# An attention and hard-swish kernel: its fallback path rolled into one loop over the batches, with a shared identity matrix

## The chip, the cores and the metric

The kernel runs on one core of a Trainium2 chip. The metric is the device time of one execution in microseconds (us), as the median of several runs. Beside it stands one profiled execution, whose span reaches from its first to its last recorded instruction.

## What is computed

The input `x` has 4 batches of 12480 rows with 128 channels; there are 32 inducing rows. The reference, cut to what matters:

```python
def mab(q, kv):
    s = scale * (q @ kv.transpose(0, 2, 1))
    s = s - s.max(-1, keepdims=True)
    a = np.exp(s)
    a /= a.sum(-1, keepdims=True) + 1e-09
    return a @ kv
h = mab(I, x)            # 32 inducing rows attend to the 12480 rows of their batch
y = mab(x, h)            # every row attends to the 32 rows of h
u = y.reshape(B * N, 128) @ w_in                       # 128 -> 2048
out = (u * np.clip(u + 3.0, 0.0, 6.0) / 6.0) @ w_out   # 2048 -> 128
```

## The kernel before

The kernel has two paths. The **main path** is straight code, without a loop at run time. It uses that a hard-swish whose argument stays between -3 and 3 is a polynomial of second degree: with the 32 rows of `h` known, the output of a row of `x` is a sum over products of its attention weights, with coefficients that are worked out once for each batch (`c_units`). A batch's 12480 rows are cut into 7 groups (6 of 128 partitions by 16 rows, one of 48 by 4), and the groups into 25 chunks of 4 rows for each partition. A loop written out in Python goes over the 100 chunks of all batches (`t` in `range(total)`); for each it issues the exponentials (`b_base`), the products (`b_prod`), the linear and the quadratic matmuls into one PSUM bank (`b_lin`, `b_quad`, the last at L692), and one chunk later the evacuation (`b_evac`, L708) and, after each group, the output DMA from SP's queue (L715). Between the parts of a chunk a list of units of the next batch is filled in by share (`fill`, `bg`). The inputs come by DMAs from GpSimd's queue (`load_x`, L118).

At the start GpSimd's queue holds the first load of `x`, the two instructions that make the identity (`make_identity`; in the profile they have lines of `masks.py`), four more loads of `x`, and then small constants. The identity is used by one transpose of the inducing rows (L173), by its copy in bf16 (`ident_b`, L162) with which all rows of `x` are transposed, and by the constant `sel` (L194).

At the end the kernel counts in how many places its conditions hold (five VectorE operations at L793 to L806, a matmul at L810, a sum at L812), compares the count with the number wanted and writes `bad_i` (L814), and evacuates the last chunk. All five engines then read `bad_i` into a register (`values_load`, the profile's L818) and branch (`tc.If`, the profile's L821). If a condition failed, they go into the **direct path** (`direct_path`): three loops of 130 tiles of 96 rows for each batch, in float32, which compute the reference as it stands. With the given inputs the conditions hold, and no instruction of the direct path runs.

How this is laid out in the instruction streams matters here. Each engine has its own stream of instructions of 64 bytes, and the order in each is: the main path; the branch into the direct path, which is not taken; a short "else" part, which sets the semaphores to what the direct path would have left them at (`EVENT_SEMAPHORE` at L821) and ends in a second branch, over the direct path to the end; the direct path; the end. In the end (the profile's L966, where the tile context closes) SP waits for every DMA queue and every engine, and then all engines meet twice: each drains and adds to a semaphore, GpSimd waits for the four others and releases them.

The direct path is written out for each batch, since `for b in range(B)` is a Python loop; only the three loops within a batch (`tc.For_i`) are loops at run time. Each of them has, on every engine, a part that is run if it has no iterations, a part between two iterations in which all engines meet and semaphores are set back, and a part behind it that waits for everything. It makes an identity of its own with two GpSimd operations. Counted in the streams that this kernel compiles to (marks of branch targets not counted), the second branch stands at, and the distance from it to the end is:

| engine | place of the second branch | instructions from it to the end | of them for one batch |
|---|---|---|---|
| TensorE | 7917 | 950 | 236 |
| VectorE | 761 | 420 | 104 |
| ScalarE | 575 | 301 | 75 |
| GpSimd | 97 | 306 | 75 |
| SyncE | 241 | 406 | 97 |

The direct path has 19 DMAs, all from SP's queue: three for the weights and the inducing rows, and four for each batch. SP gives its DMAs eight semaphores in turn, S[108] and S[112] to S[118]; the last output DMA of the main path has S[108], and the direct path begins with S[112].

Of the kernel before, what the change touches and what calls it, by code (L numbers as in the profile page):

```python
# [9 lines left out]
FP32 = mybir.dt.float32  # L10
# [30 lines left out]
def kernel(  # L41
# [8 lines left out]
    nc = tc.nc  # L50
    P = nc.NUM_PARTITIONS
    B, N, C = x.shape
# [4 lines left out]
    scale = 1.0 / math.sqrt(C)  # L57
# [18 lines left out]

    keep = ctx.enter_context(tc.tile_pool(name="keep", bufs=1))
    bad_i = keep.tile([1, 1], I32, name="bad_i")

    with ExitStack() as es:  # L80
        es.enter_context(tc.manual_schedule())
        const = es.enter_context(tc.tile_pool(name="const", bufs=1))
# [69 lines left out]
            nc.gpsimd.dma_start(w_out_r[:, :, :], w_out)  # L152


        ident = const.tile([P, P], FP32, name="ident")
        make_identity(nc, ident[:, :])
        for g in range(1, XBUF):
            load_x(0, g)
# [586 lines left out]
        for t in range(total):  # L745
            if t % NCK == 0:
                b = t // NCK
# [71 lines left out]
        bad_i[0:1, 0:1], min_val=0, max_val=1, skip_runtime_bounds_check_because="a comparison gives 0 or 1"  # L819
    )  # L820
    with tc.If(bad > 0, preferred_fallthrough_block=False):  # L821
        direct_path(tc, x, inducing, moe_w_in, moe_w_out, out, scale)


def direct_path(tc, x, inducing, moe_w_in, moe_w_out, out, scale):
    nc = tc.nc
    P = nc.NUM_PARTITIONS
    B, N, C = x.shape
    M = inducing.shape[0]
    F = moe_w_in.shape[1]  # L830
    FB = F // P
    TN = 96
    assert N % TN == 0
    xf = x.rearrange("b n c -> (b n) c")
    PSUM = bass.MemoryType.PSUM
    with ExitStack() as es:
        kp = es.enter_context(tc.tile_pool(name="d_keep", bufs=1))
        wk = es.enter_context(tc.tile_pool(name="d_work", bufs=1))
        ps = es.enter_context(tc.tile_pool(name="d_ps", bufs=1, space=PSUM))
        ident = kp.tile([P, P], FP32, name="d_ident")  # L840
        make_identity(nc, ident[:, :])
        w_in = kp.tile([P, F], FP32, name="d_w_in")
        nc.sync.dma_start(w_in[:, :], moe_w_in[:, :])
        w_out = kp.tile([P, FB, C], FP32, name="d_w_out")
        nc.sync.dma_start(w_out[:, :, :], moe_w_out.rearrange("(kb kp) c -> kp kb c", kp=P))
        I_sb = kp.tile([M, C], FP32, name="d_I")
        nc.sync.dma_start(I_sb[:, :], inducing[:, :])
        I_T = kp.tile([P, M], FP32, name="d_IT")
        tr = ps.tile([P, 512], FP32, name="d_tr")
        nc.tensor.transpose(tr[:, :M], I_sb[:, :], ident[:M, :M])  # L850
        nc.vector.tensor_copy(I_T[:, :], tr[:, :M])

        def load(row):
            xt = wk.tile([TN, C], FP32, name="d_x")
            nc.sync.dma_start(xt[:, :], xf[bass.ds(row, TN), :])
            tr = ps.tile([P, 512], FP32, name="d_tr")
            nc.tensor.transpose(tr[:, :TN], xt[:, :], ident[:TN, :TN])
            xT = wk.tile([P, TN], FP32, name="d_xT")
            nc.vector.tensor_copy(xT[:, :], tr[:, :TN])
            return xt, xT  # L860

        def weights_of(xT):
            s = ps.tile([P, 512], FP32, name="d_s")
            nc.tensor.matmul(s[:M, :TN], lhsT=I_T[:, :], rhs=xT[:, :])
            return s

        for b in range(B):
            mx = kp.tile([M, 1], FP32, name="d_mx")
            nm = kp.tile([M, 1], FP32, name="d_nm")
            D = kp.tile([M, 1], FP32, name="d_D")  # L870
            Ha = kp.tile([M, C], FP32, name="d_Ha")
            HT = kp.tile([P, M], FP32, name="d_HT")
            nc.vector.memset(mx[:, :], -3.0e38)
            nc.vector.memset(D[:, :], 0.0)
            nc.vector.memset(Ha[:, :], 0.0)
            with tc.For_i(b * N, (b + 1) * N, TN) as row:
                xt, xT = load(row)
                s = weights_of(xT)
                m1 = wk.tile([M, 1], FP32, name="d_m1")
                nc.vector.tensor_reduce(m1[:, :], s[:M, :TN], axis=AX.X, op=ALU.max)  # L880
                nc.vector.tensor_max(mx[:, :], mx[:, :], m1[:, :])
            nc.vector.tensor_scalar_mul(nm[:, :], mx[:, :], -scale)
            with tc.For_i(b * N, (b + 1) * N, TN) as row:
                xt, xT = load(row)
                s = weights_of(xT)
                a = wk.tile([M, TN], FP32, name="d_a")
                nc.scalar.activation(a[:, :], s[:M, :TN], ACT.Exp, scale=scale, bias=nm[:, 0:1])
                d1 = wk.tile([M, 1], FP32, name="d_d1")
                nc.vector.tensor_reduce(d1[:, :], a[:, :], axis=AX.X, op=ALU.add)
                nc.vector.tensor_add(D[:, :], D[:, :], d1[:, :])  # L890
                tr = ps.tile([P, 512], FP32, name="d_tr")
                nc.tensor.transpose(tr[:TN, :M], a[:, :], ident[:M, :M])
                aT = wk.tile([TN, M], FP32, name="d_aT")
                nc.vector.tensor_copy(aT[:, :], tr[:TN, :M])
                hp = ps.tile([P, 512], FP32, name="d_h")
                nc.tensor.matmul(hp[:M, :C], lhsT=aT[:, :], rhs=xt[:, :])
                nc.vector.tensor_add(Ha[:, :], Ha[:, :], hp[:M, :C])
            nc.vector.tensor_scalar_add(D[:, :], D[:, :], 1.0e-9)
            nc.vector.reciprocal(D[:, :], D[:, :])
            nc.vector.tensor_scalar_mul(Ha[:, :], Ha[:, :], D[:, 0:1])  # L900
            tr = ps.tile([P, 512], FP32, name="d_tr")
            nc.tensor.transpose(tr[:, :M], Ha[:, :], ident[:M, :M])
            nc.vector.tensor_copy(HT[:, :], tr[:, :M])
            with tc.For_i(b * N, (b + 1) * N, TN) as row:
                xt, xT = load(row)
                s = ps.tile([P, 512], FP32, name="d_s")
                nc.tensor.matmul(s[:TN, :M], lhsT=xT[:, :], rhs=HT[:, :])
                m2 = wk.tile([TN, 1], FP32, name="d_m2")
                nc.vector.tensor_reduce(m2[:, :], s[:TN, :M], axis=AX.X, op=ALU.max)
                nc.vector.tensor_scalar_mul(m2[:, :], m2[:, :], -scale)  # L910
                a = wk.tile([TN, M], FP32, name="d_a2")
                nc.scalar.activation(a[:, :], s[:TN, :M], ACT.Exp, scale=scale, bias=m2[:, 0:1])
                d2 = wk.tile([TN, 1], FP32, name="d_d2")
                nc.vector.tensor_reduce(d2[:, :], a[:, :], axis=AX.X, op=ALU.add)
                nc.vector.tensor_scalar_add(d2[:, :], d2[:, :], 1.0e-9)
                nc.vector.reciprocal(d2[:, :], d2[:, :])
                nc.vector.tensor_scalar_mul(a[:, :], a[:, :], d2[:, 0:1])
                tr = ps.tile([P, 512], FP32, name="d_tr")
                nc.tensor.transpose(tr[:M, :TN], a[:, :], ident[:TN, :TN])
                aT = wk.tile([M, TN], FP32, name="d_aT2")  # L920
                nc.vector.tensor_copy(aT[:, :], tr[:M, :TN])
                hp = ps.tile([P, 512], FP32, name="d_h")
                nc.tensor.matmul(hp[:, :TN], lhsT=Ha[:, :], rhs=aT[:, :])
                h = wk.tile([P, TN], FP32, name="d_hT")
                nc.vector.tensor_copy(h[:, :], hp[:, :TN])
                up = ps.tile([P, FB, P], FP32, name="d_u")
                for jb in range(FB):
                    nc.tensor.matmul(up[:, jb, :TN], lhsT=w_in[:, jb * P : (jb + 1) * P], rhs=h[:, :])
                g = wk.tile([P, FB, TN], FP32, name="d_g")
                nc.vector.tensor_scalar(g[:, :, :], up[:, :, :TN], 3.0, 0.0, op0=ALU.add, op1=ALU.max)  # L930
                nc.vector.tensor_scalar(g[:, :, :], g[:, :, :], 6.0, 1.0 / 6.0, op0=ALU.min, op1=ALU.mult)
                nc.vector.tensor_mul(g[:, :, :], g[:, :, :], up[:, :, :TN])
                op = ps.tile([P, 512], FP32, name="d_o")
                for jb in range(FB):
                    nc.tensor.matmul(
                        op[:TN, :C], lhsT=g[:, jb, :], rhs=w_out[:, jb, :], start=(jb == 0), stop=(jb == FB - 1)
                    )
                ot = wk.tile([TN, C], FP32, name="d_ot")
                nc.vector.tensor_copy(ot[:, :], op[:TN, :C])
                nc.sync.dma_start(out[bass.ds(row, TN), :], ot[:, :])  # L940


# [28 lines left out]
```

## Time and profile before

| what | us |
|---|---|
| median of 5 runs | 328.26 |
| lowest and highest of them | 327.68 and 330.8 |
| profiled execution, its own time | 327.56 |
| its span | 325.8 |
| TensorE busy (matmul) | 301.3 (92% of the span) |
| VectorE, ScalarE, GpSimd busy | 237.9, 229.4, 23.3 |
| mean granted TensorE clock | 0.974 |

The profiled execution took 1.8 us more than its span, which begins with the first and ends with the last instruction. Start times in the profile count from the start of the span. A letter q behind an engine (SPq) is its sequencer: waits on semaphores, branches, register loads and drains are done there and do not count as busy. Queues q8 and q14 of kind "instruction" are those by which the engines' own instructions are brought in: q8 moved 33 packets and 0.54 MB, so 16 KB each, q14 21 packets and 0.17 MB, so 8 KB each.

### The profile page before, as it was taken

The numbers are of one execution on the slowest core, as the hardware profiler recorded it, in microseconds if no ns is written. First come the engines' busy times: TensorE is split into PE (matmuls) and PEld (weight loads), VectorE is DVE, ScalarE is ACT, GpSimd is POOL, SyncE is SP. The second block draws the span as 40 slices with busy tenths as digits, with TensorE's granted clock in tenths as the row PEclk, the third lists the DMA queues.
The fourth block names the chain that finished last, engine by engine and source line by source line (L and its number), as shares of the span: only waits on it lengthen the run. The fifth ranks groups of instructions, "written<-read, shape, count | busy, mean of one in ns | idle before, by whom it ended". The sixth has DMA issues, their size and how long they took to land.

```text
span 325.8 us, 9615 instructions
## 1 busy us (share of the span) xinstructions
PE 301.3 (92%) x3920; PEld 236.3 (73%) x3934; DVE 237.9 (73%) x542; ACT 229.4 (70%) x416; POOL 23.3 (7%) x59
## 2 busy tenths in 40 slices
PE   6798998999799998999999998999999999999980
PEld 2684766888477786898777786898777787777770
DVE  2688766788486776978796776978796777887780
ACT  2582787986459858887579768888489756777720
POOL 8140210101000000110100000100000000000000
PEclk9799997999979999999999999999999999999995
DMA  7999398798855155579984256561654255666642
GB/s 234 409 300 233 76 406 296 261 313 271 330 185 167 44 186 189 150 251 359 319 301 162 65 179 195 143 201 29 195 172 160 61 184 187 196 218 208 196 185 105
DMA packets 26486, 67.78 MB, mean 208 GB/s; under 512 B 5152, under 2 KB 19520, under 8 KB 20288
## 3 DMA queue, kind: packets, MB, share of 16 engines
q1 hardware_dynamic: 18160, 38.36, 36.6%
q0 software_dynamic: 8272, 28.71, 28.3%
q8 instruction: 33, 0.54, 0.6%
q14 instruction: 21, 0.17, 0.2%
HBM read 29.77 MB, written 25.56 MB: 170 GB/s over the span
## 4 chain that ended last, share of the span: by engine, by line
PE 75%; DMA 10%; DVE 7%; ACT 3%; issue 2%; POOL 0%; SPq 0%; DVEq 0%; POOLq 0%
PE op L692 26%; PE bp L652 11%; PE op L676 7%; DMA d<-dk 6%; PE hnd L282 6%; PE pt L260 5%; PE cp L490 4%; PE dpm L470 4%; DMA xr<-in_x_dram 4%; PE s L268 2%; PE pp L623 2%; DVE xT L261 2%; PE sp L593 2%; PE ep L579 2%; DVE TD L668 2%
## 5 line engine op out<-in xcount | busy, mean ns | idle before, releaser
L659 ACT ACTIVATE TF<-bp 128x512 bf16<-128x512 f32 (+1 forms) x200 | 117.9, 600 | 40.3 <-PE rp L612 26.3
L692 PE MATMUL op<-Cq,TF 128*128 128x128 bf16 (+1 forms) x800 | 109.8, 224 | 0.0
L692 PE MATMUL op<-Cq,TD 128*128 128x128 bf16 (+1 forms) x800 | 107.0, 220 | 2.1 <-DVE TD L668 2.1
L708 DVE TENSOR_TENSOR os<-op,r_all 128x512 f32<-128x512 f32 (+1 forms) x100 | 68.3, 683 | 20.5 <-PE op L692 19.6
L692 PEld LDWEIGHTS <-TF 128*128 128x128 bf16 (+1 forms) x800 | 50.9, 98 | 34.2 <-issue 26.0
L668 DVE TENSOR_TENSOR TD<-TF,d 128x1024 bf16<-128x1024 bf16 (+1 forms) x100 | 67.0, 670 | 7.9 <-DMA d<-dk 4.0
L652 PE MATMUL bp<-xT,W 128*128 128x512 bf16 (+1 forms) x189 | 71.7, 380 | 0.0
L692 PEld LDWEIGHTS <-TD 128*128 128x128 bf16 (+1 forms) x800 | 61.9, 99 | 2.5 <-DVE TD L668 2.4
L676 PE MATMUL op<-BD,nf 128*128 128x512 f32 (+1 forms) x100 | 53.5, 535 | 0.0
L251 ACT CAST xb<-xr 128x1024 bf16<-128x1024 f32 (+1 forms) x47 | 46.0, 1002 | 7.1 <-DMA xr<-in_x_dram 7.1
L481 ACT ACTIVATE sq<-dpm 128x512 bf16<-128x512 f32 x60 | 36.5, 645 | 5.2 <-PE dpm L470 3.2
L261 DVE COPY xT<-pt 128x1024 bf16<-128x1024 bf16 (+1 forms) x56 | 33.8, 617 | 8.0 <-PE pt L260 7.8
L613 DVE RECIPROCAL r_all<-rp 128x4 f32<-128x4 f32 (+1 forms) x100 | 17.8, 178 | 24.5 <-PE rp L612 23.9
L612 PE MATMUL rp<-one,nf 128*128 128x4 f32 (+1 forms) x100 | 34.8, 348 | 0.1
L260 PE MATMUL pt<-ident_b,xb 128*128 128x128 bf16 (+1 forms) x400 | 30.9, 223 | 2.3 <-DVE xb L251 1.5
L282 PE MATMUL hnd<-xr,a 128*32 128x128 f32 x384 | 32.2, 231 | 0.5 <-ACT a L274 0.5
L282 PEld LDWEIGHTS hnd<-xr,a 128*32 128x32 f32 x384 | 26.0, 113 | 2.7 <-issue 2.1
L260 PEld LDWEIGHTS <-xb 128*128 128x128 bf16 (+1 forms) x400 | 24.6, 100 | 4.2 <-DVE xb L251 1.6
L118 POOL DMA_DIRECT2D xr<-in_x_dram x25 | 13.5, 543 | 166.2 <-ACT TF L659 97.7
L490 PE MATMUL cp<-w_out_b,sq 128*128 128x128 bf16 x256 | 24.3, 220 | 0.5 <-ACT sq L481 0.4
L630 ACT ACTIVATE dk<-pp 128x512 bf16<-128x512 f32 (+1 forms) x28 | 15.8, 564 | 11.5 <-PE pp L623 10.5
L470 PE MATMUL dpm<-dH,w_in_b 128*128 128x512 bf16 x62 | 22.9, 381 | 0.9 <-DVE dH L400 0.5
(106 smaller groups left out, 344.5 us busy)
## 6 DMA issues: line engine op xcount, KB each, us to landing
out_dram<-os SPq DMA_DIRECT2D x24, 1024.0 KB, 4.1
xr<-in_x_dram POOLq DMA_DIRECT2D x23, 1024.0 KB, 8.0
d<-dk SPq DMA_DIRECT2D x96, 128.0 KB, 4.1
xr<-in_x_dram POOLq DMA_DIRECT2D x2, 512.0 KB, 4.7
w_in_r<-in_moe_w_in_dram POOLq DMA_DIRECT2D x1, 1024.0 KB, 10.1
w_out_r<-in_moe_w_out_dram POOLq DMA_DIRECT2D x1, 1024.0 KB, 14.5
w_in_b<-in_moe_w_in_dram POOLq DMA_DIRECT2D x1, 512.0 KB, 7.1
w_out_b<-in_moe_w_out_dram POOLq DMA_DIRECT2D x1, 512.0 KB, 12.3
```

Of the source, the lines that this page charges most:

```text
L251: eng(xb[:p, lo:hi, :], xs[(b, g)][:p, lo:hi, :].bitcast(FP32))
L260: nc.tensor.transpose(pt[:, (i - lo) * p : (i - lo + 1) * p], xb[:p, i, :], ident_b[:p, :p])
L261: nc.vector.tensor_copy(st["xT"][:, t0 + lo * p : t0 + hi * p], pt[:, : (hi - lo) * p])
L282: nc.tensor.matmul(st["hnd"][:M, :C], lhsT=a1[:p, i * M : (i + 1) * M], rhs=xs[(b, g)][:p, i, :], start=(g == 0 and i == 0), stop=(g == NG ...
L481: nc.scalar.activation(sq[:, :], dpm[:, :], ACT.Square)
L490: nc.tensor.matmul(st["cp"][:, k * C : (k + 1) * C], lhsT=sq[:, k * P : (k + 1) * P], rhs=w_out_b[:, jc, :], start=(jc == 0 and k == 0), s ...
L652: nc.tensor.matmul(bp[:, :w], lhsT=st["W"][:, k].rearrange("p m i -> p (m i)"), rhs=st["xT"][:, c0 : c0 + w],)
L659: nc.scalar.activation(st[("x", c)][:, k, :w], bp[:, :w], ACT.Exp, scale=scale)
L668: nc.vector.tensor_mul(u[:, :, :w], t[:, :, :w], d[:, :w].unsqueeze(1).to_broadcast([P, 2, w]))
L676: nc.tensor.matmul(op[:p, :], lhsT=st[("nf", g)][:, j * p : (j + 1) * p], rhs=st["BD"][:, :], start=True, stop=False, skip_group_check=True,)
L692: nc.tensor.matmul(op[:p, s * C : (s + 1) * C], lhsT=T[k][:, s * p : (s + 1) * p], rhs=st["Cq"][:, k, :], start=False, stop=(s == SL - 1 a ...
L708: nc.vector.tensor_mul(ot[:p, j * SL : (j + 1) * SL, :], op[:p, :].rearrange("p (s c) -> p s c", c=C), r_all[:p, b, c, :].unsqueeze(2).to_ ...
```

## The change

The identity of the main path moves from the pool `const`, which is given back with the main path, to the pool `keep`, which stays; it is made in the same place by the same call. The direct path takes it over in place of making its own, and so issues nothing to GpSimd. Its loop over the batches becomes a loop at run time, whose register `r0` is added to the row in each load and in the output's DMA.

```diff
     keep = ctx.enter_context(tc.tile_pool(name="keep", bufs=1))
     bad_i = keep.tile([1, 1], I32, name="bad_i")
+    ident = keep.tile([P, P], FP32, name="ident")
...
-        ident = const.tile([P, P], FP32, name="ident")
         make_identity(nc, ident[:, :])
...
-        direct_path(tc, x, inducing, moe_w_in, moe_w_out, out, scale)
+        direct_path(tc, x, inducing, moe_w_in, moe_w_out, out, ident, scale)
...
-        ident = kp.tile([P, P], FP32, name="d_ident")
-        make_identity(nc, ident[:, :])
...
-        for b in range(B):
+        with tc.For_i(0, B * N, N) as r0:
...
-            with tc.For_i(b * N, (b + 1) * N, TN) as row:
-                xt, xT = load(row)
+            with tc.For_i(0, N, TN) as row:
+                xt, xT = load(r0 + row)
...
-                nc.sync.dma_start(out[bass.ds(row, TN), :], ot[:, :])
+                nc.sync.dma_start(out[bass.ds(r0 + row, TN), :], ot[:, :])
```

The edit of the loop's head and of `load` is made in all three loops of a batch.

## The prediction

> **What bounds the kernel now.** I first read the page's head and its table of DMA queues.
>
> ```profile
> span 325.8 us, 9615 instructions
> PE 301.3 (92%) x3920; PEld 236.3 (73%) x3934; DVE 237.9 (73%) x542; ACT 229.4 (70%) x416; POOL 23.3 (7%) x59
> ...
> q8 instruction: 33, 0.54, 0.6%
> q14 instruction: 21, 0.17, 0.2%
> ```
>
> TensorE bounds the run as a whole, but the change edits none of its work that runs. Of instructions that run, it moves the identity to another tile; the rest is code that is jumped over. So the place to look is the end, where that jump lies. The timeline there:
>
> ```profile
> 317.63 0.14 DVE L814 TENSOR_SCALAR bad_i<-cs 1x1 int32<-1x1 f32 x1
> 317.70 0.67 DVE L708 TENSOR_TENSOR os<-op,r_all 48x512 f32<-48x512 f32 x1
> 318.39 0.34 SPq L715 DMA_DIRECT2D out_dram<-os  x1
> ```
>
> The last work ends at 318.37 us and the last output lands 1.9 us after its issue, at 320.3. The span ends at 325.8: 5.5 us in which nothing is computed or stored. Two views by line (engine, operation, count: duration in ns, first and last start) tell what fills them, first the branches, then the end:
>
> ```profile
> L821 SPq EVENT_SEMAPHORE  x8: 17/17/17, 320.3 to 320.8; - x8
> L821 ACTq COMPARE_BRANCH  x2: 38/41/44, 318.9 to 319.1; - x2
> L821 POOLq COMPARE_BRANCH  x2: 38/44/49, 319.0 to 319.2; - x2
> L821 PEldq COMPARE_BRANCH  x2: 95/2006/3917, 319.0 to 319.3; - x2
> L821 DVEq COMPARE_BRANCH  x2: 51/53/55, 319.0 to 319.2; - x2
> L821 SPq COMPARE_BRANCH  x2: 38/44/49, 319.3 to 320.9; - x2
> ```
>
> ```profile
> L966 SPq EVENT_SEMAPHORE  x14: 17/28/28, 323.5 to 325.7; - x14
> L966 POOLq EVENT_SEMAPHORE  x4: 17/17/17, 325.0 to 325.7; - x4
> L966 POOLq DRAIN  x3: 50/107/2832, 322.1 to 325.5; - x3
> ...
> L966 ACTq DRAIN  x2: 8/54/100, 321.5 to 325.2; - x2
> L966 DVEq DRAIN  x2: 10/34/57, 322.5 to 325.2; - x2
> L966 PEldq DRAIN  x2: 8/40/73, 323.3 to 325.3; - x2
> ```
>
> Each engine's second branch (the last start at L821) is followed by its first instruction at L966 only us later. With the records' second decimals: ACT 319.10 to 321.54, POOL 319.18 to 322.10, DVE 319.22 to 322.47, PE 319.31 to 323.29, SP 320.92 to 323.54: 2.4, 2.9, 3.2, 4.0 and 2.6 us for one jump. The first branch, which falls through, is followed by the next instruction after 0.09 to 0.15 us. The DMA view from 319.5 us on shows why:
>
> ```profile
> q14 instruction: 8, 0.07, 3.3%
> q8 instruction: 2, 0.03, 2.6%
> ```
>
> These are ten fetches of instructions in 6 us, two for each engine: the block that it jumped to, and, 0.6 us after its first instruction there, the block behind it. In the 9.2 us before there is none on q14.
>
> **The fetch rule, from this trace.** In the run itself, up to 319.5 us, q8 moved 31 packets for TensorE's 7917 instructions (255 each) and q14 13 for the 1674 of the other four (129 each): blocks of 256 and 128. Each crossing of a block's edge brings one packet, the block behind the one just entered. VectorE's came when it had started 62, 188, 318, 443, 573 and 701 instructions, SyncE's at 84 and 213, ScalarE's last at 441, GpSimd's at 69, TensorE's last at about 7836. So when the jump comes, what is loaded ahead of it is: VectorE (at 761) 68 + 128 = 196, SyncE (at 241) 100 + 128 = 228, GpSimd (at 97) the same 228, ScalarE (at 575; its next edge was due, but had brought no packet yet) at least 128, TensorE (at 7917) at least 7836 + 512 - 7917 = 431. The jumps of before go 420, 406, 306, 301 and 950 instructions: all five beyond, and all five fetched.
>
> **The change, part by part.**
>
> *The loop over the batches.* One batch instead of four, so the distances become one batch's (the table above) and an outer loop's frame. By the parts of the inner loops, that frame is some 25 instructions on each engine (13 of waits behind it, 5 between iterations, 2 if empty, 5 of register and branch), on SyncE some 45 with its semaphore settings, and there about 10 additions for the addresses. With the three loads of SyncE and the few first instructions I estimate ScalarE 100, GpSimd 101, VectorE 134, SyncE 155 and TensorE 267, against limits of 128, 228, 196, 228 and 431. All fit; ScalarE is nearest its limit.
>
> *What a jump into a loaded block costs.* No such jump is in the trace. Bounds: 0.09 us (the branch that falls through) and today's 2.4 to 4.0 us. I take 0.1, since the fetch accounts for the rest: SP's packet starts 0.9 us after the branch and takes 0.4, and its first instruction starts 1.3 us behind it.
>
> [...]
>
> *SyncE.* Its eight semaphore settings begin when the last output has landed (320.35, a wait on S[108]) and end with the branch at 320.92. One batch has 3 + 4 = 7 DMAs, on S[112] to S[118]: the setting of S[108], and with it this wait, goes from the "else" part into the list of waits in the end. Then seven settings of 0.067 us from 319.43 on, the branch at 319.9, a hit at 320.0, four waits of 0.06, the landing at 320.35, the other eight waits and two drains (0.6): SP is through at about 320.95 instead of 324.36. If the wait stays where it is, 320.92 + 0.1 + 0.83 = 321.85.
>
> *GpSimd.* Without work in the direct path its setting goes too (0.08), and its DRAIN starts at about 319.2 instead of 322.10. This DRAIN took 2.832 us, to 324.93; the meeting went on at 324.98, though SP, the last of the others, was through at 324.36. So today GpSimd, not SP, ends last, by 0.6 us. What holds the DRAIN the trace does not show: no GpSimd instruction is open. Its other three took 0.18, 0.11 and 0.05. First drains are longer than second ones on the others too (ACT 0.100 and 0.008, PE 0.073 and 0.008), all after a jump with a fetch; at the start of the run, without one, they took 0.008 to 0.010. Bounds: 0.05 and 2.83. I take 2.83, its own row, as if it were a first-use cost of the drain. Then it ends at 322.05, when all others are long through.
>
> [...]
>
> *The meeting.* From GpSimd's wait at 324.98 to the end 0.80 us; unchanged.
>
> *The identity.* Same two instructions in the same place in POOL's queue (2.46 to 3.06 us), same loads behind them. Users: `ident_b` at 3.09, first wanted by the transposes at 6.75, which wait for ScalarE's cast of `x`; `I_T` at 3.65, wanted at 10.74. Cover 3.4 us, so nothing; without cover, one us for each us. Other addresses in SBUF: no row shows an address to matter; zero, with the runs' own spread (327.7 to 330.8) as its doubt.
>
> *Sum.* The span ends at 319.2 + 2.83 + 0.05 + 0.80 = 322.9 instead of 325.8: -2.9 us. The profiled execution becomes 324.7; the median lies 0.7 above that execution, so 325.4.
>
> **Rivals.**
>
> - *The drain shortens as well.* For: first drains without a fetch were short. Against: none of GpSimd's own rows is after a long rest without a fetch. Then SP ends last, and the gain is 3.1 to 4.0 us: 324.3 to 325.2.
> - *One engine still misses.* The estimates of the distances are off by a few, and ScalarE has 28 to spare. ScalarE alone costs nothing (through at 321.6); TensorE alone would be through at 323.36, end 324.2, median 326.7; GpSimd alone keeps everything: 328.2.
> - *A taken branch fetches anew wherever it goes,* even into a loaded block. The trace has no counterexample. Then the fetches stay, GpSimd's drain still starts at 322.0: 328.2, no change.
> - *Slower: the identity delays the head.* In a pool opened ahead of the scheduled part, its first writes could take a wait that they lack now. The place is POOL's queue at 2.46 us; the four loads of `x` at 3.00 stand behind it, and ScalarE's cast at 9.66 had waited 3.0 us for such a load, so each us of wait costs one us. It decides from 4.5 us on (2.9 gained and 1.6 for half a per cent). Against: nothing is queued ahead of these writes but the first load, which takes 1.2 us to issue. 330.0 and more.
>
> **How the numbers follow.** Chances: the sum as it stands 0.52, shorter drain 0.23, one engine missing 0.07 (half of it within half a per cent), no change 0.12, slower 0.06. Half a per cent, 1.6 us, is about what a measurement of this kernel can tell from no change. Faster by more: 0.52 + 0.23 + 0.03, less 0.02 for the spread of medians, 0.76; within: 0.18; slower: 0.06. The time is 325.4. The low end takes the whole of the shorter drain, less 0.3 for the spread: 324.0. The high end takes the missing engine and the spread of the runs, 327.6, which leaves out the cases without a gain, 0.18.
>
> **What would show it.** Right: in the DMA view after 318 us no more first fetches, only one packet for each engine that enters its next block, six or fewer in all; first instructions at L966 on ACT, DVE, POOL and PE before 319.6; SP's L966 waits from about 320.0, or 321.0 if S[108] stays; POOL's DRAIN of about 2.8 us from 319.2; the span 2.9 shorter, all of it behind 318.4 us. Wrong: gaps of 2 us and more at L821; a drain of 0.2 (then the second case); evacuation of the last chunk later than 318.4 (then the head moved).

## The result, and the profile after

The changed kernel takes 324.41 us as the median of 52 runs, the kernel before 328.01 us as the median of 94. The ratio of the two is 0.9949 with a 95% interval of 0.9931 to 0.9968; it compares the quicker executions of both kernels only, since executions of either scatter over 10 to 12 us. In a second series, side by side on one chip, it was 0.9872 (0.9802 to 0.9943), with medians of 323.84 and 327.82 us. The profiled execution took 324.6 us, its span 322.7.

The page's head and queue table after:

```profile
span 322.7 us, 9613 instructions
...
q8 instruction: 32, 0.52, 0.6%
q14 instruction: 17, 0.14, 0.1%
```

Five fetches fewer, one on TensorE's queue and four on the others'. The timeline around the end:

```profile
317.13 0.14 DVE L814 TENSOR_SCALAR bad_i<-cs 1x1 int32<-1x1 f32 x1
317.20 0.67 DVE L708 TENSOR_TENSOR os<-op,r_all 48x512 f32<-48x512 f32 x1
317.90 0.34 SPq L715 DMA_DIRECT2D out_dram<-os  x1
```

This execution is at L814 0.49 us earlier than that of before. Of the edits only the identity's place lies there, and its copy `ident_b` starts at 3.09 us in both; VectorE waited 2.9 us for the DMA of `d` (L668) instead of 4.0, which looks like scatter. What the change does lies behind L814. So the measure for all that follows is the time **from the start of L814 to the end of the span**: 325.78 - 317.63 = 8.15 us before, 322.73 - 317.13 = 5.59 after, 2.56 less. The branches and the end by line, as before (the end's line is now L964):

```profile
L821 SPq EVENT_SEMAPHORE  x7: 17/17/17, 319.0 to 319.4; - x7
L821 ACTq COMPARE_BRANCH  x2: 38/41/44, 318.4 to 318.6; - x2
L821 POOLq COMPARE_BRANCH  x2: 38/44/49, 318.5 to 318.6; - x2
L821 PEldq COMPARE_BRANCH  x2: 95/260/425, 318.5 to 318.8; - x2
L821 DVEq COMPARE_BRANCH  x2: 51/53/55, 318.5 to 318.7; - x2
L821 SPq COMPARE_BRANCH  x2: 38/44/49, 318.9 to 319.5; - x2
```

```profile
L964 SPq EVENT_SEMAPHORE  x14: 17/28/28, 319.9 to 322.7; - x14
L964 POOLq EVENT_SEMAPHORE  x4: 17/17/17, 321.9 to 322.6; - x4
L964 POOLq DRAIN  x3: 51/107/2817, 319.1 to 322.4; - x3
L964 SPq DRAIN  x3: 7/7/13, 320.7 to 322.1; - x3
L964 ACTq DRAIN  x2: 8/47/86, 319.0 to 322.1; - x2
L964 PEldq DRAIN  x2: 8/43/78, 319.3 to 322.2; - x2
L964 DVEq DRAIN  x2: 10/34/58, 319.3 to 322.2; - x2
```

Last start at L821 against first start at L964: the jumps take 0.43 us (ACT), 0.47 (POOL), 0.57 (DVE), 0.48 (PE) and 0.48 (SP) by the records' second decimals, instead of 2.4 to 4.0. The DMA view from 318.2 us on has five fetches of instructions where there were ten:

```profile
q14 instruction: 4, 0.03, 2.2%
q8 instruction: 1, 0.02, 1.4%
```

By the records each of them starts 0.6 to 0.7 us after an engine's first instruction of the end: that fits the block behind the one jumped into, and none stands between a branch and its target. SP has seven settings instead of eight and does not wait for the last output ahead of them; it is through at 320.78. GpSimd's first drain takes 2.82 us as before, from 319.07 on, and the meeting goes on at 321.94, 1.16 us after SP. The end is GpSimd's.

### The profile page after: what moved, and what is told of

It is laid out like the page before. It is cut to its first block, busy times and chain, and to the rows that moved or that the text cites. A ratio compares the mean times of both kernels' runs of the same rounds, so it can differ in the third digit from the quotient of the medians.

```text
span 322.7 us, 9613 instructions
## 1 busy us (share of the span) xinstructions
PE 301.1 (93%) x3920; PEld 236.3 (73%) x3934; DVE 238.2 (74%) x542; ACT 229.6 (71%) x416; POOL 23.4 (7%) x59
## 3 DMA queue, kind: packets, MB, share of 16 engines
q0 software_dynamic: 8272, 28.71, 28.5%
## 4 chain that ended last, share of the span: by engine, by line
PE 76%; DMA 10%; DVE 7%; ACT 3%; issue 2%; POOL 0%; SPq 0%; DVEq 0%; POOLq 0%
PE op L692 26%; PE bp L652 12%; PE op L676 7%; DMA d<-dk 6%; PE hnd L282 6%; PE pt L260 5%; PE cp L490 4%; PE dpm L470 4%; DMA xr<-in_x_dram 4%; PE s L268 2%; PE pp L623 2%; DVE xT L261 2%; PE sp L593 2%; PE ep L579 2%; DVE TD L668 1%
## 5 line engine op out<-in xcount | busy, mean ns | idle before, releaser
L668 DVE TENSOR_TENSOR TD<-TF,d 128x1024 bf16<-128x1024 bf16 (+1 forms) x100 | 67.0, 670 | 6.8 <-ACT TF L659 3.5
```

The costliest lines, as they stand in the source:

```text
L668: nc.vector.tensor_mul(u[:, :, :w], t[:, :, :w], d[:, :w].unsqueeze(1).to_broadcast([P, 2, w]))
```

## The experiments

Theory: the whole gain is the fetch behind the jump, and it counts only through GpSimd, whose drain of 2.8 us ends last. Rivals: the number of engines that fetch counts; the identity has a part; the gain lies elsewhere. Beside these, what the 2.8 us are. Each of the first eight runs is one profiled execution. The stretch behind L814 repeats well where no engine fetches (5.59, 5.60 and 5.61 us in three executions with the same end); a fetch itself differs from one execution to the next, between the kernel before and the run with the identity alone by 0.44 us on GpSimd (2.92 and 3.36) and by some 0.8 on ScalarE (2.4 and 3.2).

**GpSimd alone past its loaded blocks.** Idle writes ahead of the loop in the direct path:

```diff
+        pad = kp.tile([P, 1], FP32, name="d_pad")
+        for _ in range(160):
+            nc.gpsimd.memset(pad[:, :], 0.0)
         with tc.For_i(0, B * N, N) as r0:
```

> The changed kernel with idle GpSimd writes in the direct path, so that on GpSimd alone the end lies 263 instructions behind the branch, two instruction blocks on (101 in the changed kernel); the other four engines as changed. If the fetch behind the jump is what the change took away, and GpSimd's drain is what ends last: GpSimd fetches again (two packets more on q14), its drain starts 2.9 us behind its branch instead of 0.47 and takes 2.8, and from the write of bad_i (L814) to the end of the span it is 5.6 + 2.4 = 8.0 us, as before the change (8.15), though four engines jump as fast as after it. If the number of engines that fetch counts, or the other engines' waits: between, some 6 us. If the gain came from elsewhere: 5.6 us.

Measured: 9.32 us from L814 (at 319.83) to the end. GpSimd's lines at L821 and in the end:

```profile
L821 POOLq COMPARE_BRANCH  x2: 37/43/49, 321.2 to 321.4; - x2
...
L967 POOLq DRAIN  x3: 50/107/2831, 325.5 to 328.9; - x3
```

The jump took 4.07 us, the other four 0.43 to 0.57 as in the changed kernel. 5.59 + (4.07 - 0.47) + 0.10 for the setting that GpSimd has again (its two branches start 0.18 us apart instead of 0.08) makes 9.29. q14 moved five packets from the branches on, one more than in the changed kernel and not two as expected. One engine's fetch gives back the whole gain, and more, since this fetch was dearer than the 2.92 us of before. That the number of engines counts is out.

**ScalarE alone past its loaded blocks.** The same with 55 copies `nc.scalar.copy(pad[:, :], ident[:, 0:1])`.

> The changed kernel with idle ScalarE copies in the direct path, so that on ScalarE alone the end lies 157 instructions behind the branch (101 in the changed kernel). If blocks are of 128 instructions and one is loaded ahead: ScalarE's first instruction of the end comes 2.4 us behind its branch instead of 0.43, with two packets on q14 instead of one. If blocks are of 256: 0.43 us still. In either case ScalarE is through before 321.3 us on the changed kernel's clock, GpSimd's drain ends at 321.9, so from L814 to the end it stays 5.6 us: a fetch that costs nothing.

Measured: 6.09 us. ScalarE's lines:

```profile
L821 ACTq COMPARE_BRANCH  x2: 38/41/44, 323.0 to 323.2; - x2
...
L967 ACTq DRAIN  x2: 8/54/100, 326.9 to 327.2; - x2
```

157 instructions are too far: the jump took 3.71 us, with five packets on q14 from the branches on instead of four. With blocks of 256 it was expected at 0.43 us, so this run fits the blocks of 128 on q14 that the packets of the kernel before give (129 instructions each). The expectation missed the cost: the fetch took 3.7 us and not 2.4, so ScalarE was through at 326.96, 0.5 us behind GpSimd's drain (323.61 + 2.81 = 326.42), and the end moved by just that.

**An extra drain in GpSimd's queue**, when all its DMAs have been issued:

```diff
+            if t == 90:
+                nc.gpsimd.drain()
             tb = t + LEAD
```

> The changed kernel with one more drain in GpSimd's queue, at chunk 90, when its last DMA has long landed. Three theories of the 2.8 us: (a) the drain goes through the DMAs that GpSimd has issued since the last one, 33 of them, about 85 ns each: the early drain takes 2.8 us at some 207 us, beside other work, and the one at the end under 0.2; (b) it is the price of the first drain after a long while: the same picture, or 2.8 us for both; (c) it is the price of GpSimd's first instruction after a long rest: the one at the end keeps 2.8. Under (a), SyncE ends last (320.78 on the changed kernel's clock): from L814 to the end 4.45 us instead of 5.6. Under (c) 5.6.

Measured: 4.44 us. The end's drains on GpSimd and SP:

```profile
L966 POOLq DRAIN  x3: 39/107/112, 315.8 to 318.1; - x3
L966 SPq DRAIN  x3: 7/7/13, 317.4 to 317.7; - x3
```

The drain at the end took 0.112 us; SP, through at 317.52, now ends last. The extra one took 7.16 us from 203.92 on, beside the last two loads, which were still under way: by the trace the last of them landed at 209.68, 1.4 us ahead of the drain's end. So its premise, that the last DMA had long landed, did not hold, and its length says nothing on (a). This rules out (c), but not (a) from (b).

**A GpSimd instruction just ahead of the end**, `nc.gpsimd.tensor_copy(touch[:, :], r_all[:, B - 1, NCK - 1, :])` behind the last chunk.

> The changed kernel with one small GpSimd copy (128 by 4 values that VectorE writes for the last chunk) some 4 us ahead of the branch, so that GpSimd's cores have just worked when the drain comes. If the drain's 2.8 us are a waking up after the 110 us without work, it takes under 0.3 us and L814 to the end is 4.45 us. If they go by the DMAs issued, or by the drain itself, it keeps 2.8, and L814 to the end stays 5.6.

Measured: 5.60 us, the drain 2.824, though the copy had run 4.3 us ahead of it. A rest of GpSimd is not the cause.

**The extra drain earlier**, `if t == 30` instead of 90, behind 26 of GpSimd's 33 DMAs.

> The changed kernel with one more drain in GpSimd's queue, behind 26 of its 33 DMAs, at some 134 us; 7 DMAs follow. If the drain at the end goes through the DMAs since the last drain, it takes about 7 x 85 ns = 0.6 us. If it is the price of the first drain in a run, or of the first after any number of DMAs that have landed, 0.11 as in the run with the drain at chunk 90. If it is the price of a drain after a long while (180 us here, 112 in that run), up to 2.8. From L814 to the end 4.45 us in the first two cases, since SyncE is later than that.

Measured: 4.46 us. The end:

```profile
L966 POOLq DRAIN  x3: 51/107/687, 317.9 to 320.1; - x3
```

0.687 us with 7 DMAs since the last drain, 0.112 with none, 2.82 with 33. The first two give 0.575 / 7 = 0.082 us for each DMA, and 0.112 + 33 x 0.082 = 2.82 is the third to the digit. So the drain at the end goes by the number of DMAs that GpSimd has issued since its last drain, though the last of them landed over 100 us ago. Between the same two ends, shares by bytes (the 7 moved 6.39 of 28.71 MB) would give 0.71 us and by packets (928 of 8272) 0.42. A price that grows with the time since the last drain (105, 178 and 319 us) is not excluded by a run of its own, but would have to grow twice as fast in the second stretch as in the first.

The extra drain itself took 6.73 us here, from 132.87 on: a load issued at 132.97 was under way, landing at 138.48, and the next load was issued 7.2 us after it instead of 5.2 in the changed kernel. So this drain, in the middle of the loads, held back the next one by 2.0 us; at chunk 90 none follows.

**The loop alone**, with the direct path's own identity and the main path's in its old place:

```diff
-    ident = keep.tile([P, P], FP32, name="ident")
...
+        ident = const.tile([P, P], FP32, name="ident")
         make_identity(nc, ident[:, :])
...
+        ident = kp.tile([P, P], FP32, name="d_ident")
+        make_identity(nc, ident[:, :])
```

> The loop over the batches without the shared identity: the direct path makes its own with two GpSimd operations, the main path's lies in its old place. On GpSimd the end lies 106 instructions behind the branch instead of 101, still in the next block. If the loop is what gains: all five jumps at 0.43 to 0.57 us, GpSimd's setting of its semaphore is back (0.08 us), from L814 to the end 5.67 us against 5.59 of the changed kernel. If the identity has a part: up to 8.15, as before the change.

Measured: 5.70 us, all five jumps at 0.43 to 0.57. The 0.1 us over the changed kernel are GpSimd's setting: its two branches start 0.18 us apart again, and not 0.08.

**The identity alone**: the reverse, made from the kernel before.

> The kernel before with the shared identity and without GpSimd in the direct path, its batches still written out: 950, 420, 301, 301 and 406 instructions from the branch to the end. If the loop is what gains: all five fetch, jumps of 2.4 to 4.0 us, and of the 8.15 us from L814 to the end only GpSimd's setting goes, 0.08. If the identity has a part: nearer to 5.6. Up to L814 no difference either way but the spread of single executions.

Measured: 8.47 us. GpSimd's lines:

```profile
L821 POOLq COMPARE_BRANCH  x2: 37/43/49, 318.8 to 318.9; - x2
...
L964 POOLq DRAIN  x3: 51/107/2827, 322.2 to 325.6; - x3
```

All five fetch again (3.2, 3.4, 3.3, 4.0 and 2.8 us in the order ACT, POOL, DVE, PE, SP); GpSimd's jump took 3.36 instead of 2.92, which is more than the 0.10 that its missing setting saves. The loop is the gain; the shared identity is worth 0.1 us at the end by the run before this one (5.70 against 5.59) and hides in the scatter of a fetch here.

**No direct path to jump over.** `direct_path` with the one line `nc.sync.dma_start(out[0:128, :], ident[:, :])`.

> The changed kernel with a direct path of one DMA (it leaves the fallback computation out, which does not run with these inputs): the second branch jumps over 0 to 1 instructions, within a loaded block. Two readings of the 0.43 to 0.57 us that a jump into the next block takes: the price of any taken jump (then the same here, and 5.5 us from L814 to the end, the missing setting on GpSimd aside), or the price of changing the block (then about 0.1 us here, GpSimd's drain starts 0.37 earlier and it is 5.2 us).

Measured: 5.22 us. Drains in the end, by line:

```profile
L853 POOLq DRAIN  x3: 51/107/2755, 319.6 to 322.9; - x3
...
L853 ACTq DRAIN  x2: 8/8/8, 319.5 to 322.6; - x2
...
L853 PEldq DRAIN  x2: 8/8/8, 319.7 to 322.6; - x2
```

The jumps took 0.15 (ACT), 0.16 (POOL), 0.21 (DVE), 0.25 (PE) and 0.19 us (SP). So 0.3 us of the changed kernel's 0.47 on GpSimd are the change into the next, loaded block. The first drain of ACT, PE and DVE, 0.06 to 0.10 us in the kernels that change the block, is 0.008, 0.008 and 0.017 here. GpSimd's keeps its 2.8 (2.76).

**Timed, side by side on one chip.** The changed kernel, the extra drain at chunk 90, and this drain with the direct path's seven DMAs moved from SyncE's queue to GpSimd's (`nc.gpsimd.dma_start` for each `nc.sync.dma_start` in `direct_path`).

> The changed kernel again, timed beside the next two. By the profiles 2.6 us less than before from L814 to the end, so some 0.8 per cent less; the single executions lie some us apart.

> The changed kernel with GpSimd's extra drain at chunk 90, timed: 4.45 us from L814 to the end, 1.15 less than the changed kernel and 3.7 less than before: 1.1 per cent under before. If the extra drain holds something up where it stands, less.

> As the last, and the direct path's seven DMAs in GpSimd's queue instead of SyncE's. They do not run, but the semaphore settings that stand for them go to GpSimd, which has time, and SyncE, which ends last, saves seven of 0.067 us: SyncE is through 0.5 us earlier, GpSimd's own drain (0.11) at about the same time. From L814 to the end 3.95 us, 4.2 less than before: 1.3 per cent under before. If GpSimd's settings or its jump (133 instructions, within the next block) take longer than that, GpSimd ends last and it is 4.2 to 4.45.

| kernel | L814 to end, us | median, us (runs) | ratio to before, 95% interval |
|---|---|---|---|
| before | 8.15 | 327.82 (17) | |
| changed | 5.61 | 323.84 (12) | 0.9872 (0.9802 to 0.9943) |
| with the extra drain | 4.47 | 322.64 (6) | 0.9837 (0.9761 to 0.9914) |
| and the DMAs in GpSimd's queue | 4.11 | 323.27 (6) | 0.9894 (0.982 to 0.9968) |

The first column is read from one profiled execution of each kernel. All three intervals lie below 1, so all three are faster than before; by their times they cannot be told from one another, and what the extra drain and the other queue save is shown by the profiles alone. By the profile the third has the shortest end. It came out 0.16 longer than expected. Its drains on SP and GpSimd:

```profile
L966 POOLq DRAIN  x3: 39/104/107, 319.5 to 320.9; - x3
L966 SPq DRAIN  x3: 7/7/13, 320.3 to 320.6; - x3
```

SP, without settings, reached the end at 319.39 and was through its waits only 0.91 us later, not 0.76. The 0.15 are at its fifth wait, the one for the last output, which landed at 319.79: the wait was met at 319.81 us, 0.21 after the fourth and not 0.06. So what is next in the way is the landing of the last output; no run was made on it.

## Why the prediction was right, and where not

The forecast of 325.4 us, 2.9 less, and the likeliest case hold: 324.41 is 3.6 under the median of before, and behind L814 it is 2.56 us. Two agreements are luck in part. The span became 3.05 us shorter, close to the forecast, but 0.49 of it lies ahead of L814, where the forecast had nothing. And the median alone would not decide: 324.41 also lies in the range of the rival of a shorter drain (324.3 to 325.2). What decides are the rows, a drain of 2.82 us that ends 1.1 us after SP is through.

- *The fetch rule* held in every point tried: the changed kernel's 101 to 267 instructions, one distance for each engine, were hits on all five (0.43 to 0.57 us), 263 on GpSimd and 157 on ScalarE were misses (4.07 and 3.71 us). The estimates of 100, 101, 134, 155 and 267 are 101, 101, 133, 148 and 267 in the compiled streams (ScalarE, GpSimd, VectorE, SyncE, TensorE).
- *What a jump into a loaded block costs* was the term that was mis-sized: 0.1 us was taken, 0.43 to 0.57 measured. The row it was taken from, a branch that falls through, does not change the block; the run with a short path shows 0.15 to 0.25 for a taken jump within one. On GpSimd, which ends last, that is 0.37 us too little, and it explains the end's 5.59 us where the sum had 5.25 (8.15 - 2.9). The rival that a taken branch fetches anew wherever it goes falls with the same five rows.
- *SyncE*: its wait on S[108] went into the end as forecast, the settings began at 318.96, and it was through 1.11 us before GpSimd's drain ended (321.89), with 1.1 in the sum.
- *GpSimd's drain*: the value 2.83 was right (2.82), its reason was not. "A first-use cost" was argued from the other engines' first drains. Those 0.06 to 0.10 us are gone in the one run that does not change the block (8, 8 and 17 ns on ACT, PE and DVE); GpSimd's drain goes by the DMAs it has issued (0.112, 0.687 and 2.82 us behind 0, 7 and 33). The rival of a shorter drain falls, since the change issues the same 33.
- *One engine missing*: forecast that ScalarE alone costs nothing. In the run with ScalarE's padding it cost 0.5 us, since the fetch took 3.7 us and not 2.4. It did not happen in the changed kernel.
- *The identity delays the head*: no sign. `ident_b` and the loads stand where they stood, and the run with the identity alone reached L814 at 317.44 us, the kernel before at 317.63; single executions scatter by more than that.

Open is the size of the gain in device time. Behind L814 the profiles show 2.5 to 2.6 us against the one profile of the kernel before, and 2.9 against the run with the identity alone, which has the same five fetches. The first interval (1.0 to 2.3 us of 328) ends just short of that, and its ratio of 0.9949 is about the half per cent that the prediction gave as what a measurement can tell from no change; the second (1.9 to 6.5 us) holds it. Nothing in the profiles ahead of L814 was found that would take or give the difference, but single executions, which reach L814 at 313.9 to 321.7 us, could hardly show it.

## What to carry to other kernels

Code that never runs can cost time by its length alone (here 2.4 to 4.0 us for an engine's jump instead of 0.43 to 0.57, and 2.56 us of the end): look at the stretch behind the last store, compare each engine's last branch with its first instruction behind the jump, and count what lies between against the fetches seen in the trace. Of the engines that stalled there, only the one that ended last counted (GpSimd's fetch alone moved the end by 3.7 us, ScalarE's by 0.5), so undo the stalls one at a time on paper and see which one the end follows. And GpSimd's queue, which has issued 33 DMAs, had a drain of 2.82 us to pay for: have such a queue drain once when its last loads have been issued, beside other work, and not at the end. By the profiles that took 1.1 us off the end here; the device times scatter too much to show it.

## What was not expected of the hardware

- A GpSimd drain at the end, with all DMAs landed, took 0.11 us and 0.082 us for each DMA that GpSimd had issued since the last drain (0, 7 and 33 DMAs: 0.112, 0.687 and 2.82 us).
- A taken jump took 0.15 to 0.25 us within a block, 0.39 to 0.57 into the next, loaded one, and 2.4 to 4.1 with a fetch. The fetch was dearer when one engine alone had jumped past its loaded blocks: 3.71 us (ScalarE) and 4.07 (GpSimd) against 2.4 to 3.4 where all four engines of q14 had; TensorE, always alone on q8, took 3.98. The time is not in the packet: with GpSimd alone, both packets that start about 1 us after its branch had ended by 322.94, and its first instruction started at 325.47. Why was not tried.
- Up to L814, where the edits are small (the identity's place, the extra drains, the small copy), the profiled executions took from 313.9 us (the run with the drain at chunk 90) to 321.7 (the run with ScalarE's padding). The rows of the granted TensorE clock differ too, first of the one, then of the other:

```profile
PEclk9899999999999999999999999999999999999998
```

```profile
PEclk9798998999969999999999999999999999999998
```

By the trace's clock records these are 3.4 and 17.1 us at half clock ahead of L814; the kernel before had 10.2 and reached it at 317.6. It is not the whole of it: the run with the DMAs in GpSimd's queue had 13.7 us and reached L814 at 317.1. This is why the end was measured from L814 and not from the start.
